# Zeros for TensorE behind the first two score pairs only, and the sinks' transpose and row sums one step sooner

## The chip, the cores and the metric

One core of a Trainium2 chip runs the kernel. The metric is the time on the device in microseconds, from the first to the last instruction with what the launch adds around them. The profile gives the span of one execution and, for each engine (TensorE or PE with its weight loads PEld, VectorE or DVE, ScalarE or ACT, GpSimd or POOL, the DMA queue of SP), what it did when.

## What is computed

Attention with a sliding window and sinks, and then two pairs of dense layers, all in float32:

```python
scores = scale * np.matmul(q, k.transpose(0, 1, 3, 2))
keep = is_sink | in_window                  # 4 sinks, window of 128
a = softmax(np.where(keep, scores, -1e9))
x = np.matmul(a, v)                         # 2 batches, 8 heads, 768 x 64
h = x @ w_in;  g = P(h) / (Q(h) + 1e-6)     # 1536 tokens, 512 -> 2048 -> 512
x = g @ w_out
h2 = np.maximum(x @ w_in2, 0)
out = (h2 * h2) @ w_out2
```

## The kernel before, in words

The attention works in *units* u of 128 query rows (12 of them: six to a batch) and in *steps* n of two heads; a unit has four steps, n = 4u to 4u+3, and `pr` is n modulo 4. The order of the work on every engine is the order in which the code issues it (`manual_schedule`), so `step(n)` is a table that is written out by hand. One call works on several stages of several pairs of heads:

- `scores(n)` (L382): two matmuls into one of two double banks "s"; VectorE then moves in the other block (copy_predicated, L387) and adds the mask and takes the maximum (L394). They are issued two pairs at a time, at even n.
- `expo(n-1)` (L411): two exponentials on ScalarE, with the row sums `rs`.
- `trans(n-2)` (L431): two transposes into a bank "T" (two buffers); ScalarE copies them out (`pc`, L439; `ph`, L436 in the first unit of a batch), and GpSimd cuts two triangles out of them (L440, L444).
- `sinks(n-1)` at pr=0 (L422): GpSimd copies the unit's sink columns into `sk`.
- `sinks_t(u)` (L454): transposes `sk` on TensorE into a bank of its own; ScalarE casts it to `st` (L457), VectorE subtracts to get the rest (L458). The first unit of each batch has no `sk`, so nothing is done for it. `sums(u)`: ScalarE adds a small number to `rs` (L490), VectorE takes the reciprocal (L491). Both stand at pr=2, behind `trans` and ahead of `pv`.
- `xt` (L353): transposes the finished `x` of an earlier unit, at pr=0; ScalarE copies it twice (L497, L498) and GpSimd subtracts (L499).
- `pv(n-4)` (L471): the products with the values into the single bank "O", eight matmuls, or four in the first unit of a batch. At the last pair of a unit two matmuls with `st` follow (L478, L479), and VectorE multiplies the bank with `rs` into `x` (L482).
- `extra(n)`, last in a step: steps of the conversion of the dense layers' weights from raw words on VectorE (L241, L247, L253; not at pr=2), and a cast on ScalarE (L274) with a subtraction on GpSimd (L275).

In the last steps (n of 46 and more) the transposes use the "s" banks in turn, and the first projections of the dense layers (`g1`, L597) run between them; the dense layers then fill TensorE.

`fill(d, m)` (L512) issues m matmuls of zeros, 512 columns each, into a bank. 14 run ahead of everything into a bank "T". `DENSE` says how many run ahead of the scores of some pairs, into the bank of those scores: 4, 4, 3 and 3 for n = 0, 2, 4, 6, and 2 each for n = 24, 26, 28 and 30.

`setup_first` (L112 to L131) turns the two numbers n_sink and window, read as integer halves, into floats, and builds the first mask `m_0`; a cast of the four halves (L118) is its first step behind the DMA.

Of the kernel before, what the change touches and what calls it, by code (L numbers as in the profile page):

```python
# [8 lines left out]
F32 = mybir.dt.float32  # L9
# [6 lines left out]
P = 128  # L16
# [2 lines left out]
TWO32 = 4294967296.0  # L19
WS = 3  # L20
NW0 = 14
DENSE = {0: 4, 2: 4, 4: 3, 6: 3, 24: 2, 26: 2, 28: 2, 30: 2}
QP = 1.0 + 1e-6

LEAST = 2.0 ** -15 * 1.125
# [12 lines left out]
def kernel(  # L38
# [13 lines left out]
    nc = tc.nc  # L52
# [26 lines left out]
    raw = cst.tile([P, 4], I32, name="raw")  # L79
# [23 lines left out]
    def setup_first(m_0):  # L103
        ta, tb = [
            wr.tile([P, DM, 2], I32, tag="wr", name="su", bufs=NWR).rearrange("p n t -> p (n t)") for _ in range(2)
        ]
        it, it2 = ta[:, 0:2 * P], ta[:, 2 * P:3 * P]
        rel, col = ta[:, 4 * P:6 * P].bitcast(F32), ta[:, 6 * P:7 * P].bitcast(F32)
        win, snk, tmp, ge = (
            tb[:, a:b].bitcast(F32) for a, b in ((0, 2 * P), (2 * P, 3 * P), (3 * P, 4 * P), (4 * P, 6 * P))  # L110
        )
        rf, neg = tb[:, 6 * P:6 * P + 4].bitcast(F32), tb[:, 6 * P + 4:6 * P + 6].bitcast(F32)  # L112
        nc.gpsimd.iota(it, pattern=[[-1, 2 * P]], base=P, channel_multiplier=1)
        nc.gpsimd.iota(it2, pattern=[[1, P]], base=0, channel_multiplier=0)
        nc.vector.tensor_copy(rel, it)
        nc.vector.tensor_copy(col, it2)
        nc.vector.tensor_scalar(out=ge, in0=rel, scalar1=0.0, scalar2=None, op0=ALU.is_ge)
        nc.vector.tensor_copy(rf, raw)  # L118
        rv = rf.rearrange("p (j w) -> p j w", w=2)
        nc.vector.tensor_scalar(out=neg, in0=rv[:, :, 0], scalar1=0.0, scalar2=TWO32, op0=ALU.is_lt, op1=ALU.mult)  # L120
        nc.vector.scalar_tensor_tensor(out=nw, in0=rv[:, :, 1], scalar=TWO32, in1=neg, op0=ALU.mult, op1=ALU.add)
        nc.vector.tensor_tensor(out=nw, in0=nw, in1=rv[:, :, 0], op=ALU.add)
        yield
        window = lambda x: nc.vector.scalar_tensor_tensor(
            out=win[:, x], in0=rel[:, x], scalar=nw[:, 1:2], in1=ge[:, x], op0=ALU.is_lt, op1=ALU.mult
        )
        window(slice(P, 2 * P))
        nc.vector.scalar_tensor_tensor(
            out=tmp, in0=col, scalar=nw[:, 0:1], in1=win[:, P:], op0=ALU.is_lt, op1=ALU.max
        )  # L130
        addm(m_0, tmp)  # L131
        yield
        window(slice(0, P))
        nc.vector.tensor_scalar(out=snk[:, 0:SK], in0=col[:, 0:SK], scalar1=nw[:, 0:1], scalar2=None, op0=ALU.is_lt)
        yield rel, win, snk, tmp

    def setup_rest(rel, win, snk, tmp, m_1, m_2, tri):
        def addm_s(dst, src):
            nc.scalar.activation(out=dst, in_=src, func=ACTF.Identity, scale=BIG, bias=nbig)

        nc.vector.tensor_scalar(out=tri, in0=rel[:, P:], scalar1=0.0, scalar2=None, op0=ALU.is_lt)
        nc.gpsimd.tensor_tensor(out=tmp, in0=win[:, 0:P], in1=win[:, P:], op=ALU.add)
        nc.gpsimd.tensor_tensor(out=win[:, P:P + SK], in0=snk[:, 0:SK], in1=win[:, 0:SK], op=ALU.subtract)
        yield
        addm_s(m_1[:, 0:P], tmp)
        nc.scalar.activation(out=win[:, P:P + SK], in_=win[:, P:P + SK], func=ACTF.Relu)
        addm_s(m_1[:, P:], win[:, P:P + SK])
        yield
        addm_s(m_2[:, 0:P], tmp)
        addm_s(m_2[:, P:], snk[:, 0:SK])  # L150
# [40 lines left out]
    for j, (kind, m) in enumerate(jobs):  # L191
        n = 1 if kind == "v" else 1 + (wtiles[m][::2] == (0, 0)) if kind == "w" else WS + (m >= LATE)
# [88 lines left out]
    def ps_s():  # L281
        return ps.tile([P, 2, 512], F32, tag="S", name="s", bufs=2)
# [3 lines left out]
    def ps_t(tag=None, tail=False):  # L286
        if tail:
            return ps_s()[:, 0]
        if tag is None:
            tag = "U" if hq else "T"  # L290
        return ps.tile([P, 512], F32, tag=tag, name=tag, bufs=2 if tag == "T" else 1)


    def attention(ap, extra):
# [78 lines left out]
        def scores(n):  # L373
            u, pr = divmod(n, NPR)
            slots, bw, mask, co, po = geom(u)
            w = bw if po is None else 2 * bw
            t = ps_s()
            d = [t[:, e] for e in range(2)]
            fill(d[0], DENSE.get(n, 0))
            for e in range(2):  # L380
                s = slice(D * e, D * e + D)
                nc.tensor.matmul(  # L382
                    d[e][:, 0:w].rearrange("p (j n) -> p j n", n=bw),
                    lhsT=ld[u, "q"][s, pr, :], rhs=keys[s, pr, slots, 0:bw], start=True, stop=True,
                )
            if po is not None:
                nc.vector.copy_predicated(  # L387
                    out=t[:, :, co:co + P], mask=tri.unsqueeze(1).to_broadcast([P, 2, P]), data=t[:, :, po:po + P]
                )
            ns = []  # L390
            for e in range(2):
                ix = u * H + 2 * pr + e
                t = ap.tile([P, 160], F32, name="ns", bufs=6)
                nc.vector.tensor_tensor_reduce(  # L394
                    out=t[:, 0:bw], in0=d[e][:, co:co + bw], in1=mask, scale=-scale, scalar=3.0e38,
                    op0=ALU.add, op1=ALU.min, accum_out=nmax[:, ix:ix + 1],
                )
                ns.append(t)
            kps[n] = ns
# [50 lines left out]
        def sinks_t(u):  # L450
            if u not in sk:
                return
            sd = ps_t(tail=u == NU - 1)
            nc.tensor.transpose(sd[:, 0:P], sk.pop(u).rearrange("p j h s -> p (j h s)"), ident)  # L454
            st = ap.tile([P, P], F32R, name="st", bufs=2)
            hf = H * SK
            nc.scalar.copy(out=st, in_=sd[:, 0:P])  # L457
            nc.vector.tensor_tensor(out=st[hf:], in0=sd[hf:, 0:P], in1=st[hf:].bitcast(F32), op=ALU.subtract)  # L458
            sT[u] = st
# [28 lines left out]
        def sums(u):  # L488
            rs = rs_t[u]
            nc.scalar.activation(out=rs, in_=rs, func=ACTF.Identity, bias=eps)  # L490
            nc.vector.reciprocal(out=rs, in_=rs)  # L491
# [9 lines left out]
        NP = NU * NPR  # L501
# [7 lines left out]
        def fill(d, m):  # L509

            for _ in range(m):
                nc.tensor.matmul(  # L512
                    d.rearrange("p (j n) -> p j n", n=P), lhsT=wz,
                    rhs=wz.unsqueeze(1).to_broadcast([P, 4, P]), start=True, stop=True,
                )
# [11 lines left out]
        def step(n):  # L527
            nonlocal bd, moe, rest
            u, pr = divmod(n, NPR)
            if 0 <= n - 1 < NP:  # L530
                expo(n - 1)
            if n == 0:
                scores(0)
                scores(1)
                rest = setup_rest(*next(masks), m_1, m_2, tri)
                next(rest)
                sink_keys(0)
            elif n % 2 == 0 and n < NP:
                scores(n)
                scores(n + 1)  # L540
            if 0 < n < 4:
                next(rest, None)
            if n == 2:
                bd = diagonal()
                moe = setup_moe()
            if pr == 0 and u + 2 < NU:
                load(u + 2)
            if pr == 1 and n < NP and u % NB == 0:
                load_sinks(u // NB)
            if 9 <= n < 20:  # L550
                next(moe, None)
            if 0 <= n - 2 < NP:
                trans(n - 2)
            if 0 <= n - 1 < NP and pr == 0:
                sinks(n - 1)
            if (n >= 6 and pr == 2 and n < NP) or n == NP + 1:
                sinks_t(n // 4 - 1)
                sums(n // 4 - 1)
            if 12 <= n <= NP and pr == 0:
                xt(n // 4 - 3)  # L560
            if n == NP + 1:
                xt(NU - 2)
            if 0 <= n - 4 < NP:
                pv(n - 4)
            if n == NP - 2:
                g1(0)
            if pr == 2 and u % NB == 0 and 0 < u < NU:
                sink_keys(u)
            if n in (6, NB * NPR + 3):
                sink_values(u // NB, bd)  # L570
            if n in (8, NB * NPR + 4):
                sink_split(u // NB if n > 8 else 0)
            if n == NP + 4:
                xt(NU - 1)
            extra(n)
# [514 lines left out]
```

## Time and profile before

| | us |
|---|---|
| median of 3 runs | 638.39 (638.38 to 638.89) |
| the profiled execution | 638.53 |
| its span | 636.80 |
| TensorE busy | 625.2 |
| VectorE / ScalarE / GpSimd busy | 423.3 / 356.6 / 339.0 |

A row of the timeline gives start and duration in microseconds, the engine, the line, the operation, out<-in with their shapes, how many, and in brackets how long the engine sat idle before and who released it. A busy TensorE is not TensorE at its peak: its ends are modelled, and matmuls of zeros count. The attention runs up to about 110 us, the dense layers after it.

### The profile page before, as it was taken

The page shows a single profiled execution, that of the slowest core. Times are in us where ns is not written, and L with a number is a line of the kernel's source. Part 1 is how long each engine was busy: PE and PEld are TensorE (multiplying, and loading weights), DVE is VectorE, ACT ScalarE, POOL GpSimd, SP SyncE. Part 2 cuts the span into 40 slices and gives each one's busy share as a digit, 9 for nine tenths or more (in the row PEclk, how much of TensorE's full clock was granted, in tenths as well). Part 3 has the DMA queues.
Part 4 walks back from the last instruction along what each step waited for, and adds up shares of the span by engine and source line. Part 5 has one row for each costly group of instructions (what it writes and reads, how often), then busy time and mean ns, then how long its engine had stood idle before and what let it go on. Part 6 is the DMA issues. An engine that isn't in the chain of part 4 may idle for free.

```text
span 636.8 us, 9037 instructions
## 1 busy us (share of the span) xinstructions
PE 625.2 (98%) x3060; PEld 514.7 (81%) x3060; DVE 423.3 (66%) x862; ACT 356.6 (56%) x772; POOL 339.0 (53%) x343
## 2 busy tenths in 40 slices
PE   8999999999999999999999999999999999999995
PEld 6788787888888888888888888888888888888884
DVE  4887884679888888777677779869594433441321
ACT  4777877778888788697778633333242222222220
POOL 3666865667767577586567557444443132222221
PEclk9999999999999999999999999999999999999999
DMA  8846820033223233201111148737556264420101
GB/s 214 251 128 180 226 71 31 1 99 100 83 84 100 66 100 99 67 33 34 33 46 55 35 136 259 245 115 243 191 166 231 69 221 123 173 76 1 66 1 72
DMA packets 64373, 72.03 MB, mean 113 GB/s; under 512 B 15424, under 2 KB 55360, under 8 KB 64320
## 3 DMA queue, kind: packets, MB, share of 16 engines
q1 hardware_dynamic: 64176, 71.38, 36.1%
q8 instruction: 26, 0.43, 0.3%
q14 instruction: 27, 0.22, 0.1%
q10 hardware_dynamic: 144, 0.00, 0.0%
HBM read 68.23 MB, written 3.15 MB: 112 GB/s over the span
## 4 chain that ended last, share of the span: by engine, by line
PE 92%; DVE 3%; ACT 3%; issue 1%; POOL 0%; DVEq 0%; ACTq 0%
PE s L676 41%; PE T L597 34%; PE U L597 7%; PE O L471 3%; PE s L382 3%; PE T L431 1%; DVE ns L394 1%; PE T L512 1%; ACT pe L411 1%; PE s L512 1%; PE O L478 1%; DVE s L387 0%; ACT pc L439 0%; ACT xf L497 0%; PE O L479 0%
## 5 line engine op out<-in xcount | busy, mean ns | idle before, releaser
L597 PE MATMUL T<-xh,w 128*128 128x512 f32 x640 | 210.4, 390 | 0.0
L659 POOL TENSOR_TENSOR gl<-g,gh 128x512 fp32r<-128x512 f32 x48 | 62.1, 1294 | 158.0 <-ACT gh L658 157.9
L597 PEld LDWEIGHTS T<-xh,w 128*128 128x128 f32 x640 | 120.2, 188 | 25.0
L676 PE MATMUL s<-gh,w 128*128 128x512 f32 x384 | 126.3, 390 | 0.0
L597 PE MATMUL T<-xl,w 128*128 128x512 f32 x320 | 124.5, 389 | 0.0
L676 PE MATMUL s<-w,gh 128*128 128x512 f32 x384 | 118.1, 389 | 0.0
L618 POOL TENSOR_TENSOR t<-t,ah 128x512 f32<-128x512 f32 x48 | 62.3, 1297 | 41.8 <-ACT t L615 35.9
L275 POOL TENSOR_TENSOR w<-wx,w 128x512 fp32r<-128x512 f32 x64 | 82.7, 1292 | 3.2 <-ACT w L274 3.0
L676 PEld LDWEIGHTS s<-gh,w 128*128 128x128 f32 x384 | 72.1, 188 | 15.0
L676 PEld LDWEIGHTS s<-w,gh 128*128 128x128 f32 x384 | 72.1, 188 | 14.9
L659 POOL TENSOR_TENSOR gl<-t,gh 128x512 fp32r<-128x512 f32 x48 | 62.3, 1297 | 38.0 <-ACT gh L658 35.1
L658 ACT CAST gh<-g 128x512 fp32r<-128x512 f32 x48 | 29.9, 623 | 82.4 <-PE s L676 77.0
L676 PE MATMUL s<-gl,w 128*128 128x512 f32 x192 | 74.7, 389 | 0.0
L676 PE MATMUL s<-w,gl 128*128 128x512 f32 x192 | 74.7, 389 | 0.0
L597 PEld LDWEIGHTS T<-xl,w 128*128 128x128 f32 x320 | 60.1, 188 | 12.3
L647 DVE SCALAR_TENSOR_TENSOR t<-t,U 128x512 f32<-128x512 f32 x48 | 33.0, 687 | 35.9 <-ACT U L644 35.6
L658 ACT CAST gh<-t 128x512 fp32r<-128x512 f32 x48 | 29.8, 622 | 37.6 <-DVE t L651 29.3
L632 DVE TENSOR_TENSOR g<-r,T 128x512 f32<-128x512 f32 x32 | 21.8, 683 | 42.8 <-ACT r L622 42.8
L622 ACT ACTIVATE r<-T 128x512 f32<-128x512 f32 x32 | 19.1, 598 | 53.2 <-PE T L597 53.1
L471 PE MATMUL O<-vr,ph 128*128 128x64 f32 x352 | 44.6, 268 | 0.2 <-DVE x L482 0.2
L471 PEld LDWEIGHTS O<-vr,ph 128*128 128x128 f32 x352 | 43.3, 192 | 0.6 <-POOL vm L337 0.5
L274 ACT CAST w<-wx 128x512 fp32r<-128x512 f32 x64 | 39.5, 618 | 7.7 <-DVE wx L253 7.2
(152 smaller groups left out, 1065.9 us busy)
## 6 DMA issues: line engine op xcount, KB each, us to landing
wr<-in_w_in_dram SPq DMA_DIRECT2D x54, 512.0 KB, 3.7
wr<-in_w_out_dram SPq DMA_DIRECT2D x52, 512.0 KB, 3.9
qr<-in_q_dram SPq DMA_DIRECT2D x12, 256.0 KB, 4.4
keys<-in_k_dram SPq DMA_DIRECT2D x12, 256.0 KB, 4.3
vr<-in_v_dram SPq DMA_DIRECT2D x12, 256.0 KB, 4.6
wr<-in_v_dram SPq DMA_DIRECT2D x6, 512.0 KB, 4.6
out_dram<-part SPq DMA_DIRECT2D x12, 256.0 KB, 2.0
vsc<-in_v_dram SPq DMA_DIRECT2D x4, 16.0 KB
```

The source lines that it names most:

```text
L274: nc.scalar.copy(out=t[:, 0], in_=xf)
L275: nc.gpsimd.tensor_tensor(out=t[:, 1], in0=xf, in1=t[:, 0].bitcast(F32), op=ALU.subtract)
L382: nc.tensor.matmul(d[e][:, 0:w].rearrange("p (j n) -> p j n", n=bw), lhsT=ld[u, "q"][s, pr, :], rhs=keys[s, pr, slots, 0:bw], start=True, ...
L471: nc.tensor.matmul(o[:, h * D:(h + 1) * D], lhsT=pt[:, j, e], rhs=ld[u - 1 + j, "v"][:, h, :], start=(h == 0 and j == (i == 0)), stop=Fals ...
L597: nc.tensor.matmul(h, lhsT=wi[a][:, kk * P:(kk + 1) * P], rhs=(xh, xl)[b][c][:, kk, :], start=(kk == 0 and a + b == 0), stop=(kk == KD - 1 ...
L618: nc.gpsimd.tensor_tensor(out=t, in0=t, in1=ah, op=ALU.mult)
L622: nc.scalar.activation(out=r, in_=h, func=ACTF.Relu)
L632: nc.vector.tensor_tensor(out=g, in0=st.pop(k), in1=h, op=ALU.mult)
L647: nc.vector.scalar_tensor_tensor(out=t, in0=t, scalar=QP, in1=r0, op0=ALU.add, op1=ALU.mult)
L658: nc.scalar.copy(out=gh, in_=g)
L659: nc.gpsimd.tensor_tensor(out=gl, in0=g, in1=gh.bitcast(F32), op=ALU.subtract)
L676: nc.tensor.matmul(acc[L, g, c][m], lhsT=lh, rhs=rh, start=(f == f0 and a + b == 0), stop=(f == f1 and a == 1),)
```

## The change

Of the zeros, those ahead of the scores go. Five are now issued behind scores(0) and scores(1), and four behind scores(2) and scores(3), into a bank "T" in place of a score bank; the other six places have none. `sinks_t` and `sums` move from pr=2 to pr=1 of the same unit's following steps, one step sooner, and from ahead of `pv` to behind it; in the last unit they stay in step 49 but come behind `xt` and `pv`. The cast of the integer halves is left out: the three operations behind it read the integers.

```diff
-DENSE = {0: 4, 2: 4, 4: 3, 6: 3, 24: 2, 26: 2, 28: 2, 30: 2}
+DENSE = {0: 5, 2: 4}
...
-        nc.vector.tensor_copy(rf, raw)
-        rv = rf.rearrange("p (j w) -> p j w", w=2)
+        rv = raw.rearrange("p (j w) -> p j w", w=2)
...
             d = [t[:, e] for e in range(2)]
-            fill(d[0], DENSE.get(n, 0))
...
                 scores(0)
                 scores(1)
+                fill(ps_t("T"), DENSE[n])
...
             elif n % 2 == 0 and n < NP:
                 scores(n)
                 scores(n + 1)
+                if n in DENSE:
+                    fill(ps_t("T"), DENSE[n])
...
-            if (n >= 6 and pr == 2 and n < NP) or n == NP + 1:
-                sinks_t(n // 4 - 1)
-                sums(n // 4 - 1)
             if 12 <= n <= NP and pr == 0:
                 xt(n // 4 - 3)
             if n == NP + 1:
                 xt(NU - 2)
             if 0 <= n - 4 < NP:
                 pv(n - 4)
+            if 5 <= n <= NP + 1 and pr == 1:
+                sinks_t(n // 4 - 1)
+                sums(n // 4 - 1)
```

## Rows read from the trace of the kernel before

**Rows 1.** The page's 40 slices, in tenths: TensorE's busy share

```profile
PE   8999999999999999999999999999999999999995
```

**Rows 2.** Busy time by stretch (PE, PEld, DVE, ACT, POOL, clock); last row: VectorE alone

```profile
24.00:52.00 28.00, 27.21 (x216) 22.62 (x215) 23.63 (x95) 23.09 (x95) 20.05 (x39) 1.00 0.58 162
...
60.00:68.00 8.00, 7.88 (x55) 5.60 (x55) 7.08 (x27) 5.99 (x22) 5.53 (x6) 1.00 0.67 193
...
60.00:75.00 15.00, 13.43 (x52) 1.00 0.72 200
```

**Rows 3.** The chain of waits in order of time: start, us on the chain

```profile
1.12 5.96 PE T L512 x14
7.08 0.92 PE s L512 x4
8.01 0.45 PE s L382 x4
8.47 0.29 DVE ns L394
...
11.95 0.33 PE T L431
12.28 0.71 PE s L512 x3
...
14.87 0.23 PE T L431 x2
...
15.48 0.75 PE s L512 x3
...
52.29 0.46 PE s L512 x2
...
56.11 0.52 PE s L512 x2
```

**Rows 4.** Timeline: first mask, an exponential of pair 3, x of unit 5

```profile
5.17 0.17 DVE L118 CAST su<-raw 128x4 f32<-128x4 int32 x1 [2.83 <-DMA raw<-in_spans_dram]
...
6.75 0.23 DVE L101 TENSOR_SCALAR m<-su 128x128 f32<-128x128 f32 x1
...
13.97 0.39 ACT L411 ACTIVATE pe<-ns,nmax 128x128 f32<-128x128 f32 x1
...
60.21 0.69 DVE L482 TENSOR_TENSOR x<-O,rs 128x512 f32<-128x512 f32 x1 [1.43 <-PE O L479]
```

**Rows 5.** Waits by line: L478 for L458, L482 for L479 (us, times)

```profile
  PEld O L478: 1.1, 3
...
  PE O L479: 11.1, 10
```

**Rows 6.** Timeline: wait at unit 3's sinks; unit 4 around the new place

```profile
43.71 0.19 PEld L478 LDWEIGHTS O<-vsh,st 128*128 128x128 f32 x1 [0.58 <-DVE st L458]
...
47.19 0.29 POOL L422 COPY sk<-pe 128x128 f32<-128x128 f32 x1
...
47.59 0.69 DVE L241 TENSOR_SCALAR U<-wr 128x512 int32<-128x512 int32 x1
...
48.20 1.19 PE L382 MATMUL s<-keys,qr 64*128 64x272 f32 x8
...
48.67 0.36 ACT L439 COPY pc<-T 128x256 f32<-128x256 f32 x1
...
48.97 0.43 DVE L387 COPY_PREDICATED s<-tri,s 128x256 f32<-128x256 int32 x1
```

**Rows 7.** Timeline: sk of unit 7; the last unit's xt, the next projection

```profile
70.83 0.30 POOL L422 COPY sk<-pe 128x128 f32<-128x128 f32 x1
...
110.89 0.66 PE L353 MATMUL s<-ident,x 128*128 128x128 f32 x4 [0.75 <-ACT pc L439]
110.94 0.74 DVE L626 SCALAR_TENSOR_TENSOR t<-t,fa,T 128x512 f32<-128x512 f32 x1
112.19 0.48 PE L597 MATMUL T<-xh,w 128*128 128x512 f32 x1
```

More of the change, by code (lines that the diff above doesn't have):

```diff
@@ L111, in setup_first @@
         )
-        rf, neg = tb[:, 6 * P:6 * P + 4].bitcast(F32), tb[:, 6 * P + 4:6 * P + 6].bitcast(F32)
+        neg = tb[:, 6 * P:6 * P + 2].bitcast(F32)
         nc.gpsimd.iota(it, pattern=[[-1, 2 * P]], base=P, channel_multiplier=1)
```

## The prediction

> **What bounds the kernel now.** I read the page's slices first. TensorE is busy nine tenths or more in all but the first and the last [rows 1], and its granted clock is 1.00 in the stretches below [rows 2], so whatever TensorE does not issue, or does not wait for, on the chain is worth its full time, and work that is only beside it is worth nothing. Busy time alone can't say which: the zeros count as busy too. So I took the busy time by stretch next [rows 2]: from 24 to 52 us no zeros run and TensorE is still busy 27.21 of 28 us, while VectorE and ScalarE have about 5 us free each. The attention there is TensorE's; around the start of the second batch (60 to 68 us) VectorE is nearly as full. Behind the attention TensorE stays full up to the last slice [rows 1], so a microsecond won in attention comes out at the end: the other engines follow TensorE there. Then I read the chain of waits up to 112 us [rows 3], to see which of the zeros lie on it, and last the waits around the two sink matmuls [rows 5].
>
> The profiled execution took 638.53 us, its span 636.80 with 1.73 around it; that is 0.14 above the median of 638.39. The sum is made against 638.5, and about 0.1 is taken off for the median.
>
> **Zeros at the start.** The chain goes through the 14 first zeros (to 7.08), then four more in a bank of scores(0), and only then scores(0) and the mask additions at 8.47 [rows 3]. The four leave scores: 0.92 us. Five zeros now follow scores(1) and four follow scores(3). At 0.23 each (0.92 for four) that is 1.15 and 0.92 us; before, TensorE had a hole there until a bank came free and until the exponentials were done (the chain goes over VectorE, GpSimd and ScalarE from 8.47 to 11.95). Being in another bank, they wait for no reader. My walk, with estimates from these rows: scores(0), (1) 7.1 to 7.75, zeros to 8.9, scores(2), (3) to 9.6, zeros to 10.5, trans(0) to 10.9, trans(1) at 11.03, which is 11.95 less 0.92: the new zeros just fit. If they did not, they would push scores(4) back by what sticks out, at most the second 0.92.
>
> The three zeros ahead of scores(4) (0.71) and ahead of scores(6) (0.75) are on the chain too [rows 3]. Behind the first three TensorE overtakes ScalarE: trans(3) stood at 14.87 and would come at 14.87-0.92-0.71=13.24, but the last exponential of its pair starts at 13.97 and takes 0.39 [rows 4], so with ScalarE 0.92 earlier it ends near 13.45, and TensorE waits some 0.4. So 0.92+0.71+0.75-0.4, about 1.95 us at scores(8). Ends: 0.92 (ScalarE keeps the rest) and 2.4 (all of it). I take 1.95, as the chain behind scores(6) is TensorE's until scores(8).
>
> **The cast.** It takes 0.17 us [rows 4] ahead of the mask, which is done at 6.75+0.23=6.98. The first scores can be read only some 0.46 us behind their start (8.47 less 8.01), so at about 7.55 in the new order: a cover of 0.57. Worth 0; without that cover 0.17. No row shows the three small operations with an integer operand; if each cost as much again as the cast, 0.5 us would still be inside the cover.
>
> **Zeros at the second batch.** Of the four pairs those ahead of scores(24) and scores(26) are on the chain, with 0.46 and 0.52 [rows 3]. VectorE is busy 13.43 of the 15 us from 60 [rows 2], on end from x(5), which waited 1.43 us for the sink matmuls just ahead of scores(28) [rows 4]. Only these two pairs are ahead of that: 0.98 us. One more counts only if VectorE has slack that I don't see: 1.44. I take 1.0; low end 0.5, if the exponentials of steps 24 to 27 are late in place of TensorE.
>
> **The sinks' transpose one step sooner.** Its step issues one transpose on TensorE, a cast and the sums' addition on ScalarE, a subtraction and a reciprocal on VectorE; no DMA, nothing on GpSimd, so nothing passes SP's queue. It now stands behind pv(4u+1), ahead of the next pair of scores, instead of behind them and trans(4u+4). The count of instructions is the same; what goes is TensorE's weight loads waiting for the subtraction: 1.1 us in three places [rows 5], the largest 0.58 [rows 6]. There VectorE reached the subtraction only behind both score pairs; in the new order it is ahead of them. Next late would be scores(4u+8), whose banks VectorE frees, 0.5 us or more later.
>
> What it costs: the new wait is on VectorE. Take unit 4 [rows 6]. sk is ready at 47.19+0.29=47.48, TensorE's new place is 48.1 (just ahead of scores(22) at 48.20), so it does not wait. ScalarE ends the copy of trans(19) at 49.03, so the cast ends near 49.2 and adds 0.3 with the sums. VectorE is free at 47.59+0.69=48.28 and waits about 0.9 for that cast, and with L458, L491 and L247 behind it the predicated copy of scores(22) goes from 48.97 to about 50.3. Behind it: the exponentials of step 23 (0.7 later, ahead of ScalarE's next gap), and the bank for scores(25). What takes it up is VectorE's wait for the sink matmuls ahead of every x: 11.1 us in 10 units [rows 5]. At unit 3 VectorE has less time ahead of the cast, the wait is some 0.2, and the gain of 0.58 stands. At unit 7 GpSimd ends sk at 71.13 [rows 7] and the place is near 71.0: TensorE waits 0.1 to 0.3, and VectorE 0.3, in a stretch that VectorE leads; the third place's gain is used up. So 0.8 is left of 1.1, and I charge 0.25 for waits elsewhere. Ends: +1.1 gained, and 1.5 lost if the VectorE wait of five or six units shows at 0.3 each.
>
> **The last unit.** At step 49 the transpose now comes behind xt(10) and pv(45). Ahead of them it took the score bank that had been read, and xt(10) waited 0.75 us for ScalarE to read the other [rows 7]. Now xt takes the free one. But the next projection, at 112.19, needs a bank that VectorE reads until 110.94+0.75=111.69: at most 0.5 comes through. I take 0.4, ends 0 and 0.75.
>
> **Sum:** 1.95+1.0+0.8+0.4-0.25=3.9 us off 638.5, less 0.1: 634.5 us.
>
> **Rivals.** (1) *The sinks' cast takes the place of the zeros.* The 0.2 to 0.9 us that VectorE waits in each of nine units comes out on the chain in part. Half of nine times 0.6 is 2.7, so 638.4-3.9+2.7=637.2. For it: VectorE is busy 23.63 of 28 us [rows 2]; against it: the 11.1 us of idle time ahead of x [rows 5]. Chance 0.12.
>
> (2) *TensorE's clock falls.* With the zeros in place the granted clock is 1.00 from 60 to 68 us [rows 2]. The first 14 zeros took 5.96/14=0.43 us each, the next four 0.23 [rows 3]: the 1.2 GHz level costs 0.85 of a microsecond per microsecond of work. If the stretch from 60 to 68 us, where TensorE's real work is 7.88 less 0.92 of zeros, ran at the low level, it would lose 6.96x0.85=5.9 us: 638.4-3.9+5.9=640.4. It decides once more than 6 us of work run low (3.9+1.3 lost, over 0.85). For it: u=0 and u=6 have half the value products and the zeros stood just there. Against it: without zeros in their stretch, 24 to 52 us holds 1.00 [rows 2], and with the zeros gone TensorE is not emptier, its stretch is shorter. The Trainium skill, "TensorE: Matmul & The Clock Gate" (What's actually happening; Part 4: PE-mode transpose), says that the slow clock is the default, released by activity, and that transposes don't count as being busy in the same way. By that rule the stretches richest in transposes are the first to fall, and the sum would be this rival's; the rows up to 52 us don't bear it out. Chance 0.06.
>
> (3) *The zeros were only filling.* If ScalarE and VectorE set both stretches, only the first 0.92, 0.8 and 0.4 less 0.25 remain: 1.9, so 636.5. Chance 0.15. That the change doesn't do what it says: the zeros, the order and the cast are plain in the diff; 0.01.
>
> **Numbers.** The main case has 0.66, between 632.9 (2.4+1.44+1.1+0.5 off) and 636. The range reaches over rival 3 to 637.0, leaving rivals 1 and 2 and the tail below. About 0.2%, 1.3 us, is what a measurement of this kernel can tell from no change: faster than 637.1 has the main case, rival 3 and a part of rival 1, 0.84; within 0.2% the rest of rival 1 and mixed cases, 0.09; slower 0.07, mostly the clock.
>
> **What the profile after would show.** Nine zeros besides the 14, none on s; the first mask addition near 7.55; scores(8) near 16.8; no wait of L478 for st; VectorE waiting ahead of L458 and less ahead of x; xt(10) without a wait; the granted clock at 1.00. I am wrong if the clock shows less than 1.00 between 10 and 70 us, if VectorE's idle time ahead of L458 grows by more than what it loses ahead of x, or if scores(8) still starts near 18.

## The result, and the profile after

The changed kernel takes 632.97 us (median of 4 runs, 632.34 to 633.58) against 638.38 (4 runs): ratio 0.9917, with 0.99 to 0.9934 as its interval, so 5.4 us faster. 634.5 was forecast, with 632.9 as the low end: the result lies inside the range by less than 0.1 us. The profiled execution took 633.58, its span 631.8; before it was 638.53 and 636.8.

Lines of the code stand one or two lower than before, the projection one higher: scores L380, trans L429, sk L420, the sinks' transpose, cast and rest L452, L455, L456, the sink products L476 and L477, x L480, the sums L488 and L489, xt L352, zeros L510, the projection L598.

The page's slices of the kernel after, TensorE's busy share (as [rows 1]):

```profile
PE   9999999999999999999999999999999999999995
```

Busy time by stretch of the kernel after (PE, PEld, DVE, ACT, POOL, clock, DMA share, GB/s), as [rows 2]:

```profile
24.00:52.00 28.00, 28.00 (x229) 23.37 (x228) 24.11 (x97) 23.57 (x94) 20.28 (x41) 1.00 0.61 169
...
60.00:68.00 8.00, 7.27 (x51) 5.42 (x53) 6.64 (x26) 7.51 (x32) 7.50 (x12) 1.00 1.00 272
```

From 24 to 52 us TensorE has no hole left (27.21 of 28 before). From 60 to 68 us it now has 0.7 us of holes, without zeros. Its products are not slower there: eight value products take 0.84 us on the chain of waits of the kernel after, as they do in the kernel before between its zeros:

```profile
65.75 0.84 PE O L469 x8
```

```profile
58.82 0.84 PE O L471 x8
...
60.18 0.46 PE s L512 x2
```

The start of the chain of waits of the kernel after, as [rows 3]:

```profile
1.12 6.21 PE T L510 x14
7.33 0.45 PE s L380 x4
...
7.80 0.29 DVE ns L392
```

The four zeros between the first 14 and scores(0) are gone. The 14 themselves took 0.25 us longer than before.

Waits of VectorE by line in the kernel after (us in total, times, longest), as [rows 5]; no row of L476 or L477 waiting for st is left:

```profile
DVE x L480 <- PE O L477: 7.8, 7, 3.5
DVE st L456 <- ACT st L455: 4.0, 6, 1.4
...
DVE rs L489 <- ACT rs L488: 1.7, 2, 0.9
```

Timeline of the kernel after: x of units 0, 1, 3, 5, 6 and 9 (start, us):

```profile
17.22 0.69 DVE L480 TENSOR_TENSOR x<-O,rs 128x512 f32<-128x512 f32 x1
25.09 0.69 DVE L480 TENSOR_TENSOR x<-O,rs 128x512 f32<-128x512 f32 x1
...
40.79 0.69 DVE L480 TENSOR_TENSOR x<-O,rs 128x512 f32<-128x512 f32 x1
...
55.97 0.69 DVE L480 TENSOR_TENSOR x<-O,rs 128x512 f32<-128x512 f32 x1 [0.96 <-PE O L477]
...
63.99 0.69 DVE L480 TENSOR_TENSOR x<-O,rs 128x512 f32<-128x512 f32 x1
...
87.46 0.69 DVE L480 TENSOR_TENSOR x<-O,rs 128x512 f32<-128x512 f32 x1 [0.16 <-PE O L477]
```

The same multiplication (L482) started at 19.70, 28.12, 44.48, 60.21, 67.79 and 92.12 before. So the lead grows to 4.65 us by unit 9, with one loss: 4.24 at unit 5, 3.80 at unit 6.

### The profile page after: what moved, and what is told of

Read it like the earlier page. It is cut to its first block, busy times and chain, and to the rows that moved or that the text cites. A ratio compares the mean times of both kernels' runs of the same rounds, so it can differ in the third digit from the quotient of the medians.

```text
span 631.8 us, 9012 instructions
## 1 busy us (share of the span) xinstructions
PE 622.0 (98%) x3047; PEld 512.2 (81%) x3047; DVE 422.8 (67%) x861; ACT 357.0 (57%) x772; POOL 339.1 (54%) x343
## 4 chain that ended last, share of the span: by engine, by line
PE 94%; ACT 2%; DVE 1%; POOL 1%; DMA 0%; issue 0%; DVEq 0%; SPq 0%; ACTq 0%; POOLq 0%
PE s L677 41%; PE T L598 34%; PE U L598 7%; PE O L469 5%; PE s L380 3%; PE T L429 2%; PE T L510 1%; ACT pe L409 0%; PE T L352 0%; DMA vsc<-in_v_dram 0%; PE O L476 0%; PE O L477 0%; DVE ns L392 0%; POOL vm L336 0%; POOL xl L497 0%
## 5 line engine op out<-in xcount | busy, mean ns | idle before, releaser
L598 PE MATMUL T<-xh,w 128*128 128x512 f32 x640 | 210.4, 390 | 0.3 <-DVE t L627 0.3
L598 PEld LDWEIGHTS T<-xh,w 128*128 128x128 f32 x640 | 120.1, 188 | 25.4 <-DVE t L627 0.5
L598 PE MATMUL T<-xl,w 128*128 128x512 f32 x320 | 124.5, 389 | 0.0
L598 PEld LDWEIGHTS T<-xl,w 128*128 128x128 f32 x320 | 60.1, 188 | 12.4
L409 ACT ACTIVATE pe<-ns,nmax 128x136 f32<-128x136 f32 (+1 forms) x96 | 38.3, 403 | 9.2 <-DVE nmax L392 9.2
```

Of the source, the lines that this page charges most:

```text
L409: nc.scalar.activation(out=t[:, e, 0:w], in_=ns[e][:, 0:w], func=ACTF.Exp, scale=-1.0, bias=nmax[:, ix:ix + 1], accum_out=rs[:, 2 * pr + e ...
L598: nc.tensor.matmul(h, lhsT=wi[a][:, kk * P:(kk + 1) * P], rhs=(xh, xl)[b][c][:, kk, :], start=(kk == 0 and a + b == 0), stop=(kk == KD - 1 ...
```

## How the runs are compared

The time of one kernel scatters by more than 1 us between executions: 637.37 to 639.04 for the kernel before. The traces point at the start: the same 14 first zeros took 5.05 us in one run and 6.34 in another. No kernel was profiled twice, so this is read across kernels that begin alike. The chains of waits of the runs e2_order and e1_zeros:

```profile
1.12 5.05 PE T L512 x14
```

```profile
1.12 6.34 PE T L511 x14
```

Behind them the traces repeat: kernels that have the same code up to there agree to 0.02 us from the first scores to x of unit 5, and at unit 6, where GpSimd waits for a transfer, to 0.2 (x6 at -4.05 in the kernel after, -4.27 and -4.25 in e6_no_zeros and e5_sinks_load). So the table counts each start of x from the end of the 14 first zeros (row one) and gives the difference to the kernel before; "span" is counted in the same way. The later stages of the dense layers add some 0.1 to 0.3 us of their own. One profiled execution stands behind each line, the ratios below come from all runs.

| run | zeros' end | x0 | x1 | x3 | x4 | x5 | x6 | x9 | x11 | span |
|---|---|---|---|---|---|---|---|---|---|---|
| after | 7.33 | -2.73 | -3.28 | -3.94 | -3.93 | -4.49 | -4.05 | -4.91 | -5.35 | -5.25 |
| e1_zeros | 7.46 | -1.94 | -1.94 | -1.95 | -1.95 | -2.50 | -2.52 | -2.53 | -2.56 | -2.38 |
| e2_order | 6.17 | -0.95 | -1.51 | -2.16 | -2.17 | -2.21 | -1.52 | -2.38 | -2.79 | -2.69 |
| e9_sinks_alone | 6.60 | 0.00 | -0.62 | -1.32 | -1.32 | -1.36 | -1.38 | -2.30 | -2.74 | -2.42 |
| e4_sums | 7.36 | -0.93 | -0.93 | -0.58 | +0.09 | +0.10 | +0.78 | +0.66 | +0.66 | +0.92 |
| e3_cast | 6.40 | -0.42 | -0.42 | -0.42 | -0.42 | -0.42 | -0.43 | -0.09 | -0.09 | -0.02 |
| e7_zeros_back | 6.96 | -2.73 | -3.28 | -3.94 | -3.94 | -3.98 | -3.29 | -4.15 | -4.59 | -4.58 |
| e6_no_zeros | 6.80 | -2.73 | -3.28 | -3.93 | -3.93 | -4.49 | -4.27 | -5.13 | -5.55 | -5.32 |
| e5_sinks_load | 7.01 | -2.72 | -3.27 | -3.92 | -3.92 | -4.47 | -4.25 | -5.11 | -5.55 | -5.43 |
| e8_sums6 | 7.21 | -2.73 | -3.28 | -3.94 | -3.93 | -4.48 | -4.39 | -5.55 | -5.97 | -5.83 |
| e10_both | 6.70 | -2.73 | -3.28 | -3.94 | -3.93 | -4.49 | -4.39 | -5.56 | -5.99 | -5.92 |

## Experiments: the parts alone

Theory: the zeros lay on TensorE's path, and so did the stall of its sink products. Rivals: the zeros were only filling; the sinks' cast on VectorE takes the place of what goes.

**e1_zeros**, the kernel before with the zeros' change alone:

```diff
-DENSE = {0: 4, 2: 4, 4: 3, 6: 3, 24: 2, 26: 2, 28: 2, 30: 2}
+DENSE = {0: 5, 2: 4}
```

> Only the zeros change; the sinks' transpose, the row sums and the cast stay as they were. Theory (zeros sat on the chain at the start and at the second batch, and the new ones run in a hole): score pair 8 starts 1.7 us sooner than before, pair 28 another 1.0 sooner, and some of it is lost again at the second batch where the load of its sink values is late: 2.0 us off in all, with 1.5 to 2.7 as bounds, so near 636.4. Rival (the zeros were only filling, other engines set both stretches): 0.9 us off at the start and nothing behind it, near 637.5. Second rival (the new order is needed for it, since VectorE fills the hole): less than 0.7 us off.

Measured: 636.18 us, ratio 0.9966 (0.9954 to 0.9979) to 638.07, so 2.2 us. x0 and all up to x4 come 1.95 us sooner: the start is as forecast. Mask additions of pair 26 come 2.92 sooner, which is the 0.98 of two groups of zeros, but x5 only 2.50: 0.55 got through. The timeline of e1_zeros (lines one lower than before) at the last value products of unit 5 shows what took the rest:

```profile
55.82 0.41 POOL L439 TENSOR_SCALAR_AFFINE_SELECT ph<-pc 128x256 f32<-128x256 f32 x1
...
56.29 1.10 PEld L470 LDWEIGHTS O<-vr,ph 128*128 128x128 f32 x8 [0.17 <-POOL ph L439]
56.29 1.24 PE L470 MATMUL O<-vr,ph 128*128 128x64 f32 x8
...
58.09 0.69 DVE L481 TENSOR_TENSOR x<-O,rs 128x512 f32<-128x512 f32 x1 [1.50 <-PE O L478]
```

TensorE has overtaken the triangles that GpSimd cuts out of the exponentials; the products take 1.24 us where an unhindered group takes 1.00. Both rivals fall for the start. At the second batch some two fifths of the time of the first two groups was only filling, and of the other two groups nothing shows: -2.50 at x5 and -2.52 at x6.

**e2_order**, the sinks' transpose and the sums moved, all else as before; **e4_sums**, only the sums; **e9_sinks_alone**, only the sinks' transpose:

```diff
-                sinks_t(n // 4 - 1)
-                sums(n // 4 - 1)
...
+            if 5 <= n <= NP + 1 and pr == 1:
+                sinks_t(n // 4 - 1)
+                sums(n // 4 - 1)
```

In e4_sums only the second of the two calls moves, in e9_sinks_alone only the first.

> Only the sinks' transpose and the row sums move; zeros and cast stay as they were. Theory of the prediction: 0.8 + 0.4 - 0.25, about 0.95 us off. Theory formed from the trace of the changed kernel (the reciprocal is no longer directly ahead of x, the last unit wins too, and VectorE has fewer double waits): 2.5 us off, near 635.9, with the 1.36 us between pairs 8 and 12 of the changed kernel found here at least in half. Rival (the stretch from pair 8 to 12 gained from the zeros): pair 12 is sooner by less than 0.4 us and the whole gain stays under 1.2.

> Only the row sums (ScalarE's addition and VectorE's reciprocal) move to the earlier place; the sinks' transpose stays. Theory from the trace of the changed kernel (x waited a second time because the reciprocal stood directly ahead of it): the wait of about 1 us between the end of the last value products of unit 0 and its x falls to 0.1 or so, 0.5 to 1.0 us off in all, while TensorE's weight loads still wait for the sinks' rest as before (1.1 us in 3 places). Rival (the move of the sinks' transpose carries the whole gain): within 0.2 us of before, and x of unit 0 starts no sooner.

> The kernel before with the sinks' transpose, its cast and its subtraction at the new place and the row sums at the old one; zeros and cast as before. Theory (the stall of TensorE's sink products was worth 0.56, 0.64, 0.25 and 0.57 us in units 1, 3, 8 and 9, and goes with the transpose alone; the reciprocal ahead of x of unit 0 stays): units 1, 3 and 9 take 7.86 us each, unit 0 gains nothing, and 1.6 to 2.2 us are off in all, near 636.1. Rival (the two parts are needed together, since the sums alone made it slower): less than 1.0 us off.

Measured: e2_order 635.30 us, ratio 0.996 (0.9946 to 0.9974); e4_sums 639.09, ratio 1.0016 (1.0007 to 1.0026), slower; e9_sinks_alone 635.59, ratio 0.9951 (0.9937 to 0.9966). The table says where. With the sinks' transpose moved, alone or not, units 1, 3, 8 and 9 (a unit counted from the x before to its own) each lose a stall: 0.56, 0.64, 0.25 and 0.57 us in e2_order, and the last unit another 0.45 (e9_sinks_alone, where x10 is at -2.29). All units from 1 to 4 then take 7.80 to 7.86 us where 8.42 and 8.50 stood before. Moving the sums brings x0 0.9 us sooner, in both runs that have it, and costs 0.7 us at unit 6, in both as well. So e2_order (2.7 in the span) bears out the theory formed from the trace, 2.5 us, and not the prediction's 0.95. Waits by line in e4_sums and in e9_sinks_alone:

```profile
DVE rs L491 <- ACT rs L490: 7.2, 9, 1.9
PEld O L478 <- DVE st L458: 1.4, 3, 0.6
...
PE O L478 <- DVE st L458: 0.9, 2, 0.5
```

```profile
DVE x L482 <- PE O L479: 8.7, 9, 3.6
DVE st L458 <- ACT st L457: 4.9, 6, 1.9
```

In e4_sums VectorE stands 7.2 us for ScalarE's addition, comes late to the subtraction, and TensorE's weight loads wait 1.4 us for st, against 1.1 [rows 5], at other units than before: units 2 and 4, free of it before, lose 0.3 and 0.7. (The row of the products shows the same waits once more: at unit 3 of the kernel before both instructions start at 43.71.) In e9_sinks_alone VectorE waits as well (4.9 us), but the wait now lies ahead of the subtraction that TensorE needs, with most of a step to spare, and no row of L478 is left.

Not all four stalls were the sink products'. In the kernel before their weight loads wait for st in units 3, 7 and 9 (0.58, 0.26, 0.23 us). Unit 7 gains next to nothing, and units 1 and 8 have no such wait. Timeline of the kernel before in units 1 and 8:

```profile
26.17 0.44 PE L431 MATMUL T<-ident,pe 128*128 128x128 f32 x2 [0.35 <-ACT pc L439]
```

```profile
80.68 0.27 PE L454 MATMUL T<-ident,sk 128*128 128x128 f32 x1
...
81.46 0.35 ACT L439 COPY pc<-T 128x256 f32<-128x256 f32 x1
...
81.86 0.20 PEld L431 LDWEIGHTS T<-ident,pe 128*128 128x128 f32 x2 [0.20 <-ACT pc L439]
```

"The kernel before, in words" gives the sinks' transpose a bank of its own. That is wrong: as its row shows, it writes "T", one of the two banks of the transposes. At its old place the next transposes therefore need the bank of the ones just ahead of it, and wait until ScalarE has copied that out: in units 1, 8 and 9, where the copy comes late (0.35, 0.20 and 0.19 us). At the new place the next scores run in between. The waits of both kinds, 0.35, 0.58, 0.20 and 0.42 us in units 1, 3, 8 and 9, make up 1.55 of the 2.0 us gained there. In e4_sums those for the copy stay and units 1 and 8 gain nothing; in e9_sinks_alone they are gone. No run parts the bank from the cast and the subtraction, which move together.

My expectation for e4_sums was wrong in sign; the one for e9_sinks_alone left out the last unit, and laid the gain of units 1 and 8 to the wrong stall. Whether the order is better with the sums or without, the intervals don't tell.

**e3_cast**, only the cast left out:

```diff
-        nc.vector.tensor_copy(rf, raw)
-        rv = rf.rearrange("p (j w) -> p j w", w=2)
+        rv = raw.rearrange("p (j w) -> p j w", w=2)
```

> Only the cast of the integer halves is left out. Theory (the cast is covered by the zeros and the first scores): the first mask is done up to 0.2 us sooner, the first mask addition starts within 0.05 us of where it did, and the time is unchanged to 0.1 us. Rival (VectorE's queue of setup work behind the mask is what the start waits for): 0.17 us off, seen as an earlier addition for the pairs 2 to 4.

Measured: 638.53 us, ratio 1.0007 (0.9998 to 1.0016): nothing, as forecast. Its trace has x0 0.42 us sooner, since x of unit 0 does not wait there as it does in the kernel before (0.53 us for PE), and gives 0.34 back at unit 9. The same multiplication waits 0.53 in e1_zeros and e9_sinks_alone and not at all where the reciprocal stands earlier. Which event of TensorE it waits for was not found.

## Experiments: the second batch, and the clock

**e7_zeros_back**, the changed kernel with two zeros again ahead of pairs 24, 26, 28 and 30; **e6_no_zeros**, without the nine behind the first scores:

```diff
+            fill(d[0], 2 if n in (24, 26, 28, 30) else 0)
```

```diff
-DENSE = {0: 5, 2: 4}
+DENSE = {0: 0, 2: 0}
```

> The changed kernel with two zeros again ahead of score pairs 24, 26, 28 and 30, in the score bank. Theory (the zeros ahead of pairs 24 and 26 lay on the chain, but the wait for the sink values behind them takes them up in the changed kernel): pair 28 starts 0.9 to 1.0 us later, pair 34 0 to 0.5 us later, and the time grows by 0 to 0.5 us. Rival (their removal is worth its full time, as the prediction had it): 1.0 us longer, near 634.0.

> The changed kernel without the nine zeros behind the first two pairs of scores; the 14 first ones stay. Theory (the nine run in a hole of TensorE and only fill it): the same to 0.3 us, score pair 8 not more than 0.3 us sooner, the granted clock at 1.00 from 8 us on. Rival (they hold the clock up): a stretch between 8 and 20 us shows a granted clock below 1.00, and the time is 1 to 3 us longer.

Measured: e7_zeros_back 633.67 us, ratio 0.9921 (0.9907 to 0.9935) against the 0.9917 of the change; 0.51 later at x5, 0.76 at x6, 0.67 in the span. So the second batch's zeros cost 0.5 to 0.8 us here and 0.55 in e1_zeros, between theory and rival. Against e6_no_zeros and e5_sinks_load, whose unit 6 is 0.2 shorter than that of the change, it would be up to 1.0 at x6 and x9, so the rival is not excluded; but only 0.5 of it comes ahead of x5, from the two groups that the prediction counted. e6_no_zeros: 632.78 us, ratio 0.9907 (0.9893 to 0.9921), x0 to x5 the same to 0.01. The additions of pair 2, counted as in the table, come 0.6 us sooner (at -1.84; with the zeros -1.23), and by pair 6 that is gone: the nine zeros fill a hole. Busy time by stretch of e6_no_zeros (columns as above):

```profile
10.00:14.00 4.00, 3.54 (x24) 2.47 (x24) 1.82 (x10) 4.00 (x20) 2.65 (x5) 1.00 1.04 267
14.00:20.00 6.00, 6.00 (x50) 4.92 (x49) 4.96 (x20) 5.10 (x23) 3.96 (x9) 1.00 1.09 376
```

TensorE is 0.46 us idle in the first row, ScalarE not at all: it sets this stretch. The granted clock reads 1.00, and eight value products take 0.84 us on the chain here too (at 18.02).

**e5_sinks_load**, the load of the second batch's sink values at step 17; **e8_sums6**, the sums of unit 6 at their old place; **e10_both**, both:

```diff
-            if pr == 1 and n < NP and u % NB == 0:
-                load_sinks(u // NB)
+            if n in (1, 17):
+                load_sinks(n // 17)
```

```diff
+            if n == 30:
+                sums(6)
...
-                sums(n // 4 - 1)
+                if n != 29:
+                    sums(n // 4 - 1)
```

> The changed kernel with the load of the second batch's sink values issued at step 17 in place of step 25. Theory (the 1.3 us that the changed kernel loses again between pairs 28 and 34 is the wait for this load behind the transfers of step 24): GpSimd's wait ahead of the sink values' reading falls from 3.07 us to nothing, pair 34 starts 1.0 to 1.3 us sooner than in the changed kernel, and the time falls by as much, near 631.8. Rival (VectorE or ScalarE hold that stretch once the load is early): 0 to 0.4 us.

> The changed kernel, with the row sums of unit 6 (the first of the second batch, which has no sink transpose) back at their old place in step 30. Theory (what the changed kernel loses between x of unit 5 and x of unit 6 is VectorE's reciprocal waiting for ScalarE's addition of these sums, 0.9 us in one place): that wait is gone, the unit takes 7.6 us in place of 8.02, and the time falls by 0.4 to 0.7 us, near 632.4. Rival (the wait for the sink values behind it holds the stretch by itself): the unit still takes 7.9 us or more, and the time is the same to 0.2 us.

> The changed kernel with both: the row sums of unit 6 at their old place, and the load of the second batch's sink values at step 17. Theory (each of the two waits holds the stretch when the other is gone): 0.8 to 1.3 us faster than the changed kernel, near 631.9, and unit 6 at 7.4 us or less. Rival (VectorE's work in that stretch holds it): no more than the run with the sums alone, 0.4 to 0.7 us.

Measured: e5_sinks_load 633.05 us, ratio 0.9914 (0.99 to 0.9928); e8_sums6 632.59, ratio 0.9902 (0.9886 to 0.9918); e10_both 631.99, ratio 0.9892 (0.9876 to 0.9908). The chain of waits of the kernel after, and of e5_sinks_load:

```profile
54.89 2.75 DMA vsc<-in_v_dram
...
59.08 0.62 ACT vsh L346
...
60.22 0.80 ACT pe L409 x4
...
61.27 0.21 ACT rs L488
...
61.50 0.04 DVE rs L489
```

```profile
57.59 0.59 ACT xf L495
58.17 0.49 ACT xh L496
58.66 0.52 ACT vsh L346
...
59.70 0.79 ACT pe L409 x4
...
60.75 0.21 ACT rs L488
...
60.98 0.04 DVE rs L489
```

With the load early GpSimd no longer waits for it, yet the chain only changes its first links: ScalarE's casts stand in line up to the sums, and VectorE's reciprocal behind them still waits 0.7 us (0.9 after). The theory of the load fell. Even the 0.2 us at x6 may not be the edit's: e6_no_zeros, with the load in its old place, stands at the same -4.27. In e8_sums6 the reciprocal waits no more:

```profile
63.23 0.20 DVE L489 RECIPROCAL rs<-rs 128x8 f32<-128x8 f32 x1
```

Unit 6 takes 7.67 us (8.02 after, 7.80 in e5_sinks_load and e6_no_zeros, 7.58 before), unit 7 7.43 (7.73), 0.58 us in the span, or 0.51 against e6_no_zeros. So the loss of the change at unit 6 was for the most part the moved sums: VectorE, ahead of ScalarE there, waited for it a step too soon. In e10_both unit 6 takes 7.68, not 7.4, and the early load adds 0.09 to the span: by the trace the rival's size holds. By the medians e10_both is 0.98 ahead of the change, which is the theory's; they scatter too much to decide. That VectorE's work is the reason was not shown: it is busy in 6.93 of the 8 us from 56 to 64 in e10_both, 6.71 in e8_sums6, 7.18 in the kernel after.

## Experiments: a faster version

**e11_first10**, the changed kernel with 10 first zeros; **e12_best**, that with both edits of e10_both as well:

```diff
-NW0 = 14
+NW0 = 10
```

> The changed kernel with 10 zeros ahead of everything in place of 14. Theory (the first mask is done a full 1.0 us ahead of the first addition, so the first scores wait for zeros alone): the four zeros that go, at 0.23 to 0.43 us each, bring the first scores 0.9 to 1.5 us forward, the addition then waits for the mask, and the time falls by 0.8 to 1.0 us, near 632.1. Rival (the first products after the zeros then run at the slow rate that most of the 14 show, 0.43 us each, until TensorE has worked as long as before): 0 to 0.4 us.

> The changed kernel with 10 first zeros, the row sums of unit 6 at their old place and the load of the second batch's sink values at step 17. Theory (the three are in different places and add up): 0.67 us for the second batch and 0.4 to 0.9 us for the start, since the first addition comes at 6.8 us in place of 7.2 to 7.9; near 631.5, and at most 631.9. Rival (the earlier start is given back, because a transfer that the later steps wait for comes no sooner): near 632.0, with score pair 8 no sooner against the first addition than in the changed kernel, but a wait for a transfer behind it.

Measured: e11_first10 632.18 us (632.11 to 632.36), ratio 0.9896 (0.9881 to 0.9912); e12_best 631.93, ratio 0.991 (0.9897 to 0.9924) to a median of 637.92, on another chip than the other experiments. The first addition starts at 6.77 us in e11_first10, 1.0 sooner than in the profile of the change, 0.4 to 1.2 sooner than in the seven kernels with its start and 14 zeros. The chain of waits of e11_first10 no longer begins with zeros, and the timeline shows what the addition waited for last:

```profile
0.83 4.16 DMA raw<-in_spans_dram
5.02 0.18 DVE su L119
...
6.38 0.24 DVE m L101
...
6.77 0.29 DVE ns L392
```

```profile
6.14 0.72 PE L380 MATMUL s<-keys,qr 64*128 64x128 f32 x8 [0.59 <-DMA keys<-in_k_dram]
...
6.77 0.29 DVE L392 CUSTOM_DVE_ANT_0 ns<-s,m 128x128 f32<-128x128 f32 x1 [0.15 <-PE s L380]
```

The mask is done at 6.62, and VectorE then waits 0.15 us more for the first scores, which TensorE began 0.59 late because it waited for the transfer of the keys. So the keys set the start, with the mask 0.15 behind them: of the cast's 0.17 next to nothing would count. The theory's end, a wait for the mask, did not come about, though its size did. In e12_best the chain itself begins with the transfer of the keys:

```profile
1.32 4.63 DMA keys<-in_k_dram
...
6.08 0.63 PE s L380 x4
```

```profile
6.08 0.84 PE L380 MATMUL s<-keys,qr 64*128 64x128 f32 x8 [0.33 <-DMA keys<-in_k_dram]
```

The first eight products take 0.84 us here, against 0.72 in e11_first10 and 0.71 in the change: the slow rate that the rival of e11_first10 named shows in e12_best, at a price of 0.1 us at most, and not in e11_first10. x11 is 0.44 us earlier than in e10_both, of which the span shows 0.2. Whether the earlier start is given back the times don't tell, nor do they separate e12_best from e10_both. The median of e10_both is about 1 us ahead of that of the changed kernel; e12_best has its own kernel before, and by its ratio (0.991, against 0.9917 for the change) nothing is shown to be won.

## Why the prediction was right, and where its steps were off

The sum was 3.9 us; the table has 5.25 for the change, and 5.4 in the medians. The range held, but its low end was built on zeros worth 3.8 us (2.4 + 1.44), and they gave some 2.5; what carried the result there was the sinks' transpose and the reciprocal. That it held so narrowly is in part luck. Step by step:

- **Zeros at the start**, 1.95: measured 1.94 (e1_zeros). The first addition was forecast at 7.55; it stands at 7.80, which is 7.55 with the first zeros 0.25 us longer.
- **Zeros at the second batch**, 1.0: mis-sized, 0.55 (e1_zeros) to 0.7 (the span of e7_zeros_back). The step that failed was counting both groups in full. The low end (0.5) was named for late exponentials; in e1_zeros it was GpSimd's triangles behind them that were late. The reading that only two groups are on the chain was wrong as well: the chain has the one ahead of scores(28), at 60.18, too. It was left out of the sum for another reason, VectorE, and e1_zeros bears that out.
- **The sinks' transpose**, 0.8: mis-sized, 0.55 + 0.65 + 0.25 + 0.56 = 2.0 us in units 1, 3, 8 and 9. The three places of the wait for the subtraction (1.1, [rows 5]) were rightly read, and that of unit 7 is used up, as argued. What the step left out is the transposes' wait for a bank that the sinks' transpose had taken, in units 1, 8 and 9: I had looked only at the two sink matmuls. The unit times say it at once: 8.42, 7.86, 8.50 before, 7.87 after.
- **New waits**, charged with 0.25: VectorE's wait in unit 4 was forecast at about 0.9 and is 0.84 in the trace, and costs nothing, as argued. The loss came where the working had nothing to move, in unit 6, which has sums but no sink transpose: 0.44 us net of x5 to x6 (0.2 in e5_sinks_load and e6_no_zeros, 0.7 in e2_order).
- **The reciprocal**, not in the sum: moved from directly ahead of x of unit 0, it brought about 0.8 us there (x0 at -2.73, with 1.89 of it from pair 6). This step was missing; how much of it is the reciprocal's own stays open, since e3_cast has half of it without the move.
- **The last unit**, 0.4: measured 0.45, with xt(10) free of its wait and the projection behind it waiting 0.32 for VectorE.
- **The cast**, 0: measured 0.

Of the rivals, the granted clock read 1.00 in every stretch read, with no zeros in the second batch and none behind the first scores. As it also reads 1.00 over slow products at the start (below), the products' own times count for more: they are the same. The Trainium skill, "TensorE: Matmul & The Clock Gate" (Part 4: PE-mode transpose), says that transposes don't count as being busy in the same way; by that, stretches rich in transposes would be the first to fall, and no run here shows it. The wait of VectorE did take back up to 0.4 us, not 2.7. One of my signs was badly chosen: VectorE's idle time ahead of the subtraction grew by 4.0 us, and by 1.7 ahead of the reciprocal, while that ahead of x fell by less, from 11.6 (11.1 [rows 5] and the 0.5 at unit 0) to 7.8. By that sign I was wrong, and the kernel is faster all the same: most of this idle time lies off the path, where it has no price.

## What to carry to other kernels

Read a stall from the period of the loop (8.42 against 7.86 us) before adding up rows of waits: they show one wait on two engines, and a step that moves can have held up others by the bank that it took. When two small steps move together, ask of each where it alone would wait: here one carried most of the gain, and the other, alone, won at unit 0 and lost at units 2, 4 and 6. When several kernels differ by 1 us, line their traces up behind the part that scatters.

## What the runs showed of the hardware

- The same 14 zeros took 5.05 to 6.34 us in the traces of twelve kernels, and such a spread would make up most of the scatter (637.37 to 639.04). Early zeros start 0.43 us apart (512 columns in 0.43 us are 1.2 per ns, the level of 1.2 GHz), later ones 0.23; in e2_order they are fast from about 4.6 us, in e1_zeros all 14 are slow. With 10 zeros, where the keys set the start, four executions of e11_first10 lie within 0.25 us; the five of e12_best do not (631.59 to 633.50). The granted clock of e1_zeros reads 1.00 in this stretch too (busy time by stretch, columns as above), so it does not show the slow start; the distances do.

```profile
5.00:6.00 1.00, 1.00 (x4) 0.71 (x4) 0.86 (x5) 0.00 (x0) 0.00 (x0) 1.00 1.14 342
6.00:7.00 1.00, 1.00 (x4) 0.65 (x2) 0.73 (x3) 0.00 (x0) 0.00 (x0) 1.00 1.17 331
```

  The Trainium skill, "TensorE: Matmul & The Clock Gate" (What's actually happening), says that the number of slow products differs from run to run. These traces agree: some 9 of the 14 are slow in e2_order, all 14 in e1_zeros.
- An addition of ScalarE moved one step ahead made VectorE wait 7.2 us in 9 places, for a step that itself takes 0.3 us: its place in ScalarE's line is what made VectorE wait, not its length.
